# Attention products of batches 2 to 4: one fixed order, raised priority, and projections that start with both of their banks

## The chip, the cores and the metric

One core of one Trainium2 chip runs the kernel. The metric is the device time of one execution in microseconds; lower is better. Three runs of the kernel before gave 902.72, 903.56 and 904.33 us, median 903.56 us.

## The reference

The computation is a linear-attention layer with random features, followed by two dense layers without bias that share one token matrix.

```python
def _attn_ref(q, k, v, omega):            # q, k, v: (4, 8, 576, 64), omega: (128, 64)
    scale = 1.0 / np.sqrt(np.sqrt(D))
    def phi(x):
        proj = np.einsum('bhsd,md->bhsm', x, omega)
        h = proj - np.sum(x * x, axis=-1, keepdims=True) / 2.0
        h = h - np.max(h, axis=-1, keepdims=True)
        return np.exp(h) / np.sqrt(m)
    q_p, k_p = phi(q * scale), phi(k * scale)
    kv = np.einsum('bhsm,bhsd->bhmd', k_p, v)
    z = np.sum(k_p, axis=2)
    num = np.einsum('bhsm,bhmd->bhsd', q_p, kv)
    den = np.einsum('bhsm,bhm->bhs', q_p, z)[..., None] + 1e-06
    return num / den
...
x = attn_out.transpose(0, 2, 1, 3).reshape(2304, 512)
h = x @ w_in;  x = (h * np.clip(h + 3.0, 0.0, 6.0) / 6.0) @ w_out        # first layer, d_ff 2048
h = x @ w2_in; x = (h / (1.0 + np.exp(-1.702 * h))) @ w2_out              # second layer
```

## The kernel before, in words

The four batches are numbered b = 0 to 3 in the code; "batch 2 to 4" in the name of the change are b = 1 to 3. A batch has 576 tokens, handled as 4 blocks of 128 and a rest of 64, the "leftover"; the leftovers of two heads share a tile.

**Attention of one batch** (class `Att`) is a list of steps, and each step is a burst of small products on TensorE. For head h:

- `PJ(h)`, through `project` (L282): the features of k and q. Eight fp32 products with 64 contraction rows each. The two halves of the rows of TensorE work at the same time on two products, one half writing into the first of two PSUM banks and the other into the second; `project` emits second bank, first bank, second bank, and so on, each queued behind the last. VectorE then takes the maxima of each bank (L295), ScalarE the exponentials (L297).
- `QT(h)` (L366): four 128x128 transposes of the q features into one bank, copied out by ScalarE.
- `KV(h)` (L341): ten products of 128 rows by 64 columns that make the 128x65 state into one bank; two products side by side use the two halves of the columns.
- `NU(h)` (L377): eight or ten products of the same 128x64 shape, numerator and denominator into one bank; VectorE divides.
- `XT(i)` (L429): four transposes of a finished pair of heads, whose result is split by ScalarE and VectorE into the operand of the first layer. `PL`, `QTL`, `XTL` do the like for the leftover.

In the trace an fp32 product appears as two records, so a `project` is 16 records, a `KV` 20, a `NU` 16 or 20, a set of transposes 4.

**The first layer** runs in units of one batch n and one 128-wide chunk c of d_ff, 16 units a batch. `emit_h` (L504) makes twelve products of 512 columns at L513 into one bank. ScalarE (L524) and VectorE (L525) form the gate value, ScalarE (L529) and VectorE (L530) split it in two. `emit_o` (L541) comes two units later and makes twelve products at L555 into the four accumulation banks. I call the products of L513 and L555 layer products.

**How the two meet.** Attention of batch n + 1 is interleaved with the layer products of batch n: `side()` (L765) is called four times a unit, and every second call pops attention steps from a list at an even pace. The other call, and the hooks "gate" and "next", place the conversion of the weights and the sums for the second layer on ScalarE, VectorE, GpSimd and the DMA queue. After batch n's units the list is emptied. The attention of batch 0 comes first and has no layer beside it.

**Banks.** Of PSUM's eight banks, four (pool `acc`) belong to the accumulators of `emit_o` and four (pool `psp`, tag "ps") to all else; from b = 1 on, every attention step and every `emit_h` takes its banks from those four.

**What sets the order in the queues.** The program text isn't the order on an engine. The framework's scheduler builds each engine's queue ahead of time over a model of its own: whenever an engine is free in that model it takes the instruction that is ready there and stands first in priority, which is the order of the text. "Ready" includes that a bank is free. `issue_after` (in `behind`, L115) forces an instruction behind a given one of the same engine; `tc.high_priority(offset=n)` ranks an instruction as if it stood n places earlier. On the chip each engine then works through its queue in that order and waits where the data isn't there.

**Order of the steps of one batch** (`att_steps`, L450). With `b >= PAIRED`, the paired order, head h gives `PJ(h)`, for even h from 4 on `XT`, then `QT(h-1)`, then `NU(h-2)` and `KV(h-1)` as one step. Otherwise `PJ(h)`, `NU(h-2)`, `QT(h-1)`, `KV(h-1)` are steps of their own, and `XT` follows for odd h. `PAIRED` is 2, so b = 2 and 3 have the paired order and b = 1 the other.

After the first layer come the two pairs of batches of the second (L856, L873, L1008), which the change doesn't touch.

Of the kernel before, what the change touches and what calls it, by code (L numbers as in the profile page):

```python
# [22 lines left out]
def performer_moe_kernel(  # L23
# [13 lines left out]
    nc = tc.nc  # L37
# [10 lines left out]
    SL = lv.shape[1] // 2  # L48
# [7 lines left out]
    WARM = 8  # L56
    FIRST = 4
    ASIDE = 2
    PAIRED = 2
    HELD = 8  # L60
    AT_X = (0, 0, 0, 0)
    AT_XL = 32
# [23 lines left out]
    ident = const.tile([P, P], F32, name="ident")  # L86
# [28 lines left out]
    def behind(*ins):  # L115
        stack = ExitStack()
        for i in ins:
            if i is not None:
                stack.enter_context(tc.issue_after(i.ins))
        return stack  # L120
# [158 lines left out]
        nc.scalar.copy(hi, ps)  # L279
        nc.vector.tensor_tensor(out=lo, in0=ps, in1=hi.bitcast(F32), op=ALU.subtract)  # L280

    def project(a, ps):  # L282

        last = None
        for n in range(4):
            for half in (1, 0):
                rows = HALVES[half]
                with behind(last):
                    last = nc.tensor.matmul(  # L289
                        out=ps[half][:, n, :], lhsT=a(rows, n), rhs=omt[rows, :], start=True, stop=True  # L290
                    )

# [9 lines left out]
    class Att:  # L302
# [10 lines left out]
        def PL(self):  # L313
            a, self.vl = lqkv.pop(self.b)
            self.el = at.tile([P, 2 * NPAIR, M], F32, tag="el", name="el")
            ps = [bank([P, NPAIR, M], "ps") for _ in HALVES]
            project(lambda rows, i: a[rows, i, :], ps)
            for j, p in enumerate(ps):
                features(p, self.el[:, j * NPAIR:(j + 1) * NPAIR])

        def QTL(self):
            ps = bank([P, NPAIR, P], "ps")
            for i in range(NPAIR):
                nc.tensor.transpose(ps[:, i, :], self.leftover(i, 0), ident)
            self.qtl = at.tile([P, NPAIR, P], F32, tag="qtl", name="qtl")
            nc.scalar.copy(self.qtl, ps)
            shape = [P, NPAIR, D] if self.aside else [SL, NPAIR, 2 * D]
            self.xln = at.tile(shape, F32, tag=f"xln{self.aside}", name="xln")

        def PJ(self, h):  # L330
            a = qkv[self.b, h // 2][0][:, h % 2]
            ps = [bank([P, R, M], "ps") for _ in HALVES]
            project(lambda rows, n: a[rows, n // 2, n % 2, :], ps)
            self.e[h] = at.tile([P, 2, R, M], F32, tag="e", bufs=2, name="e")
            for half, p in enumerate(ps):
                self.feat[h] = features(p, self.e[h][:, half])
# [4 lines left out]
        def KV(self, h):  # L341
            i = h // 2
            vv = qkv[self.b, i][1]
            ps = bank([P, D + 1], "ps")
            for r in range(R):
                for m0 in (0, 64):
                    nc.tensor.matmul(  # L347
                        out=ps[m0:m0 + 64, :],
                        lhsT=self.feature(h, 0, r)[:, m0:m0 + 64],
                        rhs=vv[:, h % 2, r, :],  # L350
                        start=(r == 0),
                        stop=False,
                    )
            for m0 in (0, 64):
                nc.tensor.matmul(
                    out=ps[m0:m0 + 64, :],
                    lhsT=self.leftover(i, 1)[:, m0:m0 + 64],
                    rhs=self.vl[:, h % 2, i, :],
                    start=False,
                    stop=True,  # L360
                )
            kv = at.tile([P, D + 1], F32, tag="kv", bufs=4, name="kv")
            nc.scalar.copy(kv, ps)
            self.kv[h] = kv

        def QT(self, h):  # L366
            ps = bank([P, R, P], "ps")
            for r in range(R):
                nc.tensor.transpose(ps[:, r, :], self.feature(h, 1, r), ident)  # L369
            t = at.tile([P, R, P], F32, tag="qpt", bufs=2, name="qpt")  # L370
            if self.b == 0:
                nc.vector.tensor_copy(t, ps)
            else:
                nc.scalar.copy(t, ps)
            self.qt[h] = t

        def NU(self, h):  # L377
            i = h // 2
            t = self.qt.pop(h)
            kv = self.kv[h]  # L380
            if h % 2 == 0:
                self.xt[i] = at.tile([P, R, 2, D], F32, tag="xt", bufs=1, name="xt")
            ps = bank([P, 6, D + 1], "ps")
            for r in range(R):
                for s0 in (0, 64):
                    nc.tensor.matmul(  # L386
                        out=ps[s0:s0 + 64, r, :],
                        lhsT=t[:, r, s0:s0 + 64],
                        rhs=kv,
                        start=True,  # L390
                        stop=True,
                    )
            if h % 2:
                for e in range(2):
                    nc.tensor.matmul(
                        out=ps[HALVES[e], R, :] if self.aside else ps[0:SL, R + e, :],
                        lhsT=self.qtl[:, i, HALVES[e]],
                        rhs=self.kv.pop(2 * i + e),
                        start=True,
                        stop=True,  # L400
                    )
            dst = self.xt[i][:, :, h % 2, :]
            if h % 2 and self.aside:
                self.norm(ps[:, 0:R + 1, :], (dst, self.xln[:, i:i + 1, :]), P)
                return
            self.norm(ps[:, 0:R, :], (dst,), P)
            if h % 2:
                self.norm(ps[0:SL, R:R + 2, :], (self.xln[:, i].rearrange("p (h d) -> p h d", h=2),), SL)
# [20 lines left out]
        def XT(self, i):  # L429
            t = self.xt.pop(i)  # L430
            ps = bank([P, R, P], "ps")
            for r in range(R):
                nc.tensor.transpose(ps[:, r, :], t[:, r].rearrange("p h d -> p (h d)"), ident)
            o = ps.rearrange("p r s -> p (r s)")
            split(self.x[:, 0, i, :], self.x[:, 1, i, :], o)

        def XTL(self):
            ps = bank([P, NPAIR, SL], "ps")
            for i in range(NPAIR):
                if self.aside:  # L440
                    for e in HALVES:
                        nc.tensor.matmul(
                            out=ps[e, i, :], lhsT=self.xln[e, i, :], rhs=ident[e, e], start=True, stop=True
                        )
                else:
                    nc.tensor.transpose(ps[:, i, :], self.xln[:, i], ident[0:SL, 0:SL])
            c0 = self.b * SL
            nc.scalar.copy(self.xl[:, :, c0:c0 + SL], ps)

# [300 lines left out]
                prefetch_w()  # L750
    banks[0] = "ps"

    units = [(n, c) for n in range(B) for c in range(NC)]
    fetches = [
        (n * NC + u, k_, c)
# [489 lines left out]
```

## Time and profile before

| what | value |
|---|---|
| median of 3 runs | 903.56 us (902.72 to 904.33) |
| the profiled execution | 906.58 us |
| its span, first to last instruction | 904.8 us |
| PE busy | 886.0 us (98%) |
| VectorE, ScalarE, GpSimd busy | 554.3, 478.0, 322.6 us |
| mean granted TensorE clock | 0.998 of full |

The rows come from the profiled execution. PE is TensorE's products, PEld its weight loads, DVE VectorE, ACT ScalarE, POOL GpSimd, SP the engine that issues DMAs. An instruction's line number is that of the kernel before. The ends of products are modelled, so how long a burst holds TensorE is best read from its start to the start of what comes next.

### The profile page before, as it was taken

The page shows a single profiled execution, that of the slowest core. Times are in us where ns is not written, and L with a number is a line of the kernel's source. Part 1 is how long each engine was busy: PE and PEld are TensorE (multiplying, and loading weights), DVE is VectorE, ACT ScalarE, POOL GpSimd, SP SyncE. Part 2 cuts the span into 40 slices and gives each one's busy share as a digit, 9 for nine tenths or more (in the row PEclk, how much of TensorE's full clock was granted, in tenths as well). Part 3 has the DMA queues.
Part 4 walks back from the last instruction along what each step waited for, and adds up shares of the span by engine and source line. Part 5 has one row for each costly group of instructions (what it writes and reads, how often), then busy time and mean ns, then how long its engine had stood idle before and what let it go on. Part 6 is the DMA issues. An engine that isn't in the chain of part 4 may idle for free.

```text
span 904.8 us, 16525 instructions
## 1 busy us (share of the span) xinstructions
PE 886.0 (98%) x6344; PEld 757.1 (84%) x6344; DVE 554.3 (61%) x952; ACT 478.0 (53%) x973; POOL 322.6 (36%) x257
## 2 busy tenths in 40 slices
PE   8899999999999999999999999999999999999998
PEld 6667777788788778878888888878999888899998
DVE  5887688473754736475573343666887343368785
ACT  5887677376664666656553343444545232245452
POOL 0122222044636565475673121877000243440000
PEclk9999999999999999999999999999999999999999
DMA  6677669698888987778857325999889644565562
GB/s 209 226 248 270 234 239 316 245 329 282 286 275 288 342 304 290 233 276 288 314 204 256 128 98 206 349 400 356 277 288 354 233 170 162 180 174 153 158 204 82
DMA packets 74416, 224.57 MB, mean 248 GB/s; under 512 B 7521, under 2 KB 13793, under 8 KB 74337
## 3 DMA queue, kind: packets, MB, share of 16 engines
q1 hardware_dynamic: 73872, 223.12, 71.1%
q8 instruction: 50, 0.82, 0.4%
q10 hardware_dynamic: 464, 0.39, 0.2%
q14 instruction: 30, 0.24, 0.1%
HBM read 160.57 MB, written 62.91 MB: 247 GB/s over the span
## 4 chain that ended last, share of the span: by engine, by line
PE 82%; DVE 8%; ACT 6%; issue 1%; POOL 1%; DMA 1%; DVEq 0%; SPq 0%; ACTq 0%; POOLq 0%
PE o L1008 19%; PE o L555 18%; PE ps L513 18%; PE h L856 16%; PE hl L873 3%; PE ps L289 2%; ACT e L297 2%; DVE w L236 2%; PE ps L386 1%; PE ps L347 1%; ACT wtop L213 1%; DVE mx L295 1%; DVE wtop L221 1%; PE ps L369 1%; DVE gs L530 1%
## 5 line engine op out<-in xcount | busy, mean ns | idle before, releaser
L513 PE MATMUL ps<-x,wss 128*128 128x512 f32 x768 | 195.5, 399 | 2.5 <-ACT el L297 1.1
L1008 PE MATMUL o<-wss,gs 128*128 128x256 f32 x1512 | 173.9, 277 | 0.2 <-DVE gs L977 0.2
L1008 PEld LDWEIGHTS o<-wss,gs 128*128 128x128 f32 x1512 | 173.4, 188 | 0.9 <-DVE gs L977 0.6
L513 PEld LDWEIGHTS ps<-x,wss 128*128 128x128 f32 x768 | 140.9, 189 | 35.0 <-ACT wss L239 3.1
L856 PE MATMUL h<-xo,wss 128*128 128x512 f32 x672 | 158.5, 391 | 0.9 <-DVE t L889 0.9
L856 PEld LDWEIGHTS h<-xo,wss 128*128 128x128 f32 x672 | 123.9, 188 | 27.5 <-DVE t L889 1.8
L228 POOL TENSOR_TENSOR w<-w,wpow 128x1024 f32<-128x1024 f32 x32 | 69.2, 2162 | 204.6 <-DVE wpow L225 166.7
L525 DVE SCALAR_TENSOR_TENSOR ga<-ga,ps 128x512 f32<-128x512 f32 x80 | 50.1, 632 | 121.1 <-ACT ga L524 121.1
L899 POOL TENSOR_TENSOR g<-g,c 128x512 f32<-128x512 f32 x48 | 64.7, 1349 | 164.0 <-ACT g L898 163.8
L976 ACT CAST gs<-g 128x512 fp32r<-128x512 f32 x112 | 69.6, 622 | 80.3 <-PE o L1008 49.3
L555 PE MATMUL o<-gs,wsh 128*128 128x512 f32 (+1 forms) x480 | 110.4, 374 | 1.2 <-ACT gs L529 1.0
L555 PE MATMUL o<-gs,wss 128*128 128x512 f32 (+1 forms) x480 | 109.5, 374 | 0.2 <-ACT gs L529 0.2
L253 POOL TENSOR_TENSOR wsn<-w,wsn 128x512 fp32r<-128x512 f32 x64 | 86.6, 1367 | 63.5 <-ACT wsn L252 63.5
L977 DVE TENSOR_TENSOR gs<-g,gs 128x512 fp32r<-128x512 f32 x112 | 79.9, 716 | 33.6 <-ACT gs L976 32.3
L524 ACT ACTIVATE ga<-ps,three 128x512 f32<-128x512 f32 x80 | 51.4, 650 | 86.5 <-PE ps L513 86.0
L555 PEld LDWEIGHTS o<-gs,wsh 128*128 128x128 f32 x480 | 82.2, 188 | 17.6 <-ACT gs L529 1.4
L555 PEld LDWEIGHTS o<-gs,wss 128*128 128x128 f32 x480 | 82.4, 188 | 15.8 <-ACT gs L529 0.4
L297 ACT ACTIVATE e<-ps,mx 128x128 f32<-128x128 f32 x220 | 61.1, 396 | 23.5 <-DVE mx L295 23.3
L530 DVE TENSOR_TENSOR gs<-ga,gs 128x512 fp32r<-128x512 f32 x80 | 62.5, 791 | 16.5 <-ACT gs L529 14.7
L898 ACT ACTIVATE g<-c 128x512 f32<-128x512 f32 x48 | 30.3, 632 | 60.2 <-DVE c L889 60.2
L529 ACT CAST gs<-ga 128x512 fp32r<-128x512 f32 x80 | 46.0, 580 | 27.8 <-DVE ga L525 27.4
L252 ACT CAST wsn<-w 128x512 fp32r<-128x512 f32 x64 | 38.3, 620 | 39.5 <-DVE w L236 13.2
(132 smaller groups left out, 1102.7 us busy)
## 6 DMA issues: line engine op xcount, KB each, us to landing
wss<-left SPq DMA_DIRECT2D x56, 512.0 KB, 3.9
wss<-ws0i SPq DMA_DIRECT2D x48, 512.0 KB, 4.9
wraw<-in_w_in_dram SPq DMA_DIRECT2D x32, 512.0 KB, 5.4
wraw<-in_w_out_dram SPq DMA_DIRECT2D x32, 512.0 KB, 6.3
left<-wsn SPq DMA_DIRECT2D x32, 512.0 KB, 3.7
wss<-ws0o SPq DMA_DIRECT2D x24, 512.0 KB, 4.6
ws0i<-wss SPq DMA_DIRECT2D x16, 512.0 KB, 3.3
wss<-sumsa SPq DMA_DIRECT2D x16, 512.0 KB, 3.5
```

What stands on the lines that cost most here:

```text
L228: nc.gpsimd.tensor_tensor(out=w, in0=w, in1=q, op=ALU.mult)
L253: nc.gpsimd.tensor_tensor(out=s[:, :, 1], in0=t, in1=s[:, :, 0].bitcast(F32), op=ALU.subtract)
L297: act = nc.scalar.activation(out=e[:, r, :], in_=ps[:, r, :], func=AF.Exp, bias=mx[:, r:r + 1])
L513: nc.tensor.matmul(out=ps, lhsT=w[:, wi, kk, :], rhs=x[:, xi, kk, :], start=(m == 0), stop=(m == 3 * NK - 1),)
L524: nc.scalar.activation(out=g, in_=ps, func=AF.Relu, bias=three)
L530: gate[1] = nc.vector.tensor_tensor(out=s[:, 1, :], in0=g, in1=s[:, 0, :].bitcast(F32), op=ALU.subtract)
L555: nc.tensor.matmul(out=ps[:, e, :], lhsT=w[:, wi, cols], rhs=s[:, gi, :], start=(c == 0 and m == 0 and e == 0), stop=(c == NC - 1 and m == ...
L856: nc.tensor.matmul(out=ps, lhsT=s[:, wi, q, :], rhs=xop[q, op][:, xi], start=(first and m == 0), stop=(m == 5), skip_group_check=not first,)
L899: mul = eng.tensor_tensor(out=g, in0=g, in1=src, op=ALU.mult)
L976: split_ins[0] = nc.scalar.copy(hi, g)
L977: split_ins[1] = nc.vector.tensor_tensor(out=lo, in0=g, in1=hi.bitcast(F32), op=ALU.subtract)
L1008: last_row[0] = nc.tensor.matmul(out=out, lhsT=s[:, gi, d * P:(d + 1) * P], rhs=w[:, wi, :], start=(start and m == 0), stop=(stop and m == 2),
```

## The change

Three things, all in the attention of b = 1 to 3; the switch `queued[0]` is None while batch 0's attention is emitted.

- Every TensorE instruction of the attention goes through a new helper `mm`. It queues the instruction behind the attention instruction before it, so that they stand on TensorE in the order of the program among themselves (layer products may still stand between them), and ranks it 40 places earlier.
- In `project`, for b > 0, ScalarE first copies one column of a constant into the first bank and then, queued behind that, one into the second. The products overwrite both, so each waits for the copies, and the first product starts only when both banks are to be had. The copies have no raised rank.
- `PAIRED` goes from 2 to 1: b = 1 takes the paired order too.

```diff
-    PAIRED = 2
+    PAIRED = 1
+    RAISE = 40
...
-    def project(a, ps):
+    queued = [None]
+
+    def mm(f, *a, **args):
+        if queued[0] is None:
+            return f(*a, **args)
+        with behind(*queued[0]), tc.high_priority(offset=RAISE):
+            queued[0] = [f(*a, **args)]
+        return queued[0][0]
+
+    def project(a, ps, both=False):

         last = None
+        if both:
+            with behind(nc.scalar.copy(ps[0][:, 0, 0:1], three)):
+                nc.scalar.copy(ps[1][:, 0, 0:1], three)
         for n in range(4):
             for half in (1, 0):
                 rows = HALVES[half]
                 with behind(last):
-                    last = nc.tensor.matmul(
+                    last = mm(
+                        nc.tensor.matmul,
                         out=ps[half][:, n, :], lhsT=a(rows, n), rhs=omt[rows, :], start=True, stop=True
                     )
...
-            project(lambda rows, i: a[rows, i, :], ps)
+            project(lambda rows, i: a[rows, i, :], ps, self.b > 0)
...
-                nc.tensor.transpose(ps[:, i, :], self.leftover(i, 0), ident)
+                mm(nc.tensor.transpose, ps[:, i, :], self.leftover(i, 0), ident)
...
-                    nc.tensor.matmul(
+                    mm(
+                        nc.tensor.matmul,
                         out=ps[m0:m0 + 64, :],
...
+    queued[0] = []
     units = [(n, c) for n in range(B) for c in range(NC)]
```

The cut parts wrap the remaining products of `PJ`, `KV`, `QT`, `NU`, `XT` and `XTL` in `mm` in the same way.

## Rows read from the trace of the kernel before

**Rows 1.** The page's first part: engine, busy us (share of span), instructions.
```profile
PE 886.0 (98%) x6344; PEld 757.1 (84%) x6344; DVE 554.3 (61%) x952; ACT 478.0 (53%) x973; POOL 322.6 (36%) x257
```

**Rows 2.** Windows: stretch, length, busy us by engine, PEclk granted clock, DMA share, GB/s.
```profile
53.90:175.00 121.10, 119.24 (x856) 92.36 (x856) 89.09 (x181) 86.02 (x169) 27.90 (x13) 1.00 0.74 261
175.00:293.00 118.00, 117.85 (x895) 95.09 (x895) 67.38 (x114) 72.92 (x162) 60.16 (x51) 1.00 0.81 284
293.00:411.00 118.00, 115.91 (x877) 92.55 (x876) 66.98 (x112) 72.38 (x162) 65.58 (x56) 0.99 0.81 289
318.00:320.00 2.00, 2.00 (x6) 1.51 (x7) 0.58 (x1) 2.00 (x9) 1.92 (x3) 0.51 0.85 288
```

**Rows 3.** Timeline of PE, projections: start, us, engine, line, out<-in, shapes, records.
```profile
53.94 0.48 PE L289 MATMUL ps<-omt,lqk 64*128 64x128 f32 x2
...
226.24 1.16 PE L289 MATMUL ps<-omt,qk 64*128 64x128 f32 x16
227.33 0.73 PE L555 MATMUL o<-gs,wsh 128*128 128x512 f32 x2
...
338.16 0.48 PE L289 MATMUL ps<-omt,qk 64*128 64x128 f32 x2
338.58 3.06 PE L555 MATMUL o<-gs,wss 128*128 128x512 f32 x12
341.56 1.16 PE L289 MATMUL ps<-omt,qk 64*128 64x128 f32 x14
342.65 0.66 PE L369 MATMUL ps<-ident,e 128*128 128x128 f32 x4
...
387.58 0.48 PE L289 MATMUL ps<-omt,qk 64*128 64x128 f32 x2
```

**Rows 4.** Timeline of PE: one head of b = 1, then one of b = 2.
```profile
78.24 0.69 PE L386 MATMUL ps<-kv,qpt 128*64 128x65 f32 x16
78.86 0.66 PE L369 MATMUL ps<-ident,e 128*128 128x128 f32 x4
...
80.37 0.69 PE L347 MATMUL ps<-v,e 128*64 128x65 f32 x16
...
81.11 2.57 PE L513 MATMUL ps<-x,wss 128*128 128x512 f32 x10
...
213.62 0.69 PE L386 MATMUL ps<-kv,qpt 128*64 128x65 f32 x16
...
214.82 0.48 PE L289 MATMUL ps<-omt,qk 64*128 64x128 f32 x2
```

**Rows 5.** Timeline of PE, b = 1: a numerator cut by layer products.
```profile
156.35 0.57 PE L386 MATMUL ps<-kv,qpt 128*64 128x65 f32 x12
156.85 2.60 PE L513 MATMUL ps<-x,wss 128*128 128x512 f32 x10
159.38 0.34 PE L386 MATMUL ps<-kv,qpt 128*64 128x65 f32 x4
159.65 1.20 PE L555 MATMUL o<-gs,wss 128*128 128x512 f32 x4
```

**Rows 6.** Timeline of PE: twelve layer products after transposes, before other layer products.
```profile
376.67 2.99 PE L513 MATMUL ps<-x,wss 128*128 128x512 f32 x12
379.50 1.30 PE L555 MATMUL o<-gs,wsh 128*128 128x512 f32 x5
```

**Rows 7.** Timeline of PE and DVE, start of b = 3; in brackets idle before, and releaser.
```profile
311.59 0.48 PE L289 MATMUL ps<-omt,qk 64*128 64x128 f32 x2
...
314.82 0.67 DVE L525 SCALAR_TENSOR_TENSOR ga<-ga,ps 128x512 f32<-128x512 f32 x1
...
315.55 1.16 PE L289 MATMUL ps<-omt,qk 64*128 64x128 f32 x14 [0.74 <-DVE ga L525]
...
317.82 4.61 PE L513 MATMUL ps<-x,wss 128*128 128x512 f32 x12 [1.11 <-ACT el L297]
```

**Rows 8.** Groups by line and shape, ACT, 53.9 to 411 us: busy us, mean ns.
```profile
L363 ACT COPY kv<-ps 128x65 f32<-128x65 f32 x24 | 5.4, 225 | 3.7 <-PE ps L355 3.5
```

More of the change, by code (lines that the diff above doesn't have):

```diff
@@ L332, in PJ @@
             ps = [bank([P, R, M], "ps") for _ in HALVES]
-            project(lambda rows, n: a[rows, n // 2, n % 2, :], ps)
+            project(lambda rows, n: a[rows, n // 2, n % 2, :], ps, self.b > 0)
             self.e[h] = at.tile([P, 2, R, M], F32, tag="e", bufs=2, name="e")
@@ L354, in KV @@
             for m0 in (0, 64):
-                nc.tensor.matmul(
+                mm(
+                        nc.tensor.matmul,
                     out=ps[m0:m0 + 64, :],
@@ L368, in QT @@
             for r in range(R):
-                nc.tensor.transpose(ps[:, r, :], self.feature(h, 1, r), ident)
+                mm(nc.tensor.transpose, ps[:, r, :], self.feature(h, 1, r), ident)
             t = at.tile([P, R, P], F32, tag="qpt", bufs=2, name="qpt")
@@ L385, in NU @@
                 for s0 in (0, 64):
-                    nc.tensor.matmul(
+                    mm(
+                        nc.tensor.matmul,
                         out=ps[s0:s0 + 64, r, :],
@@ L394, in NU @@
                 for e in range(2):
-                    nc.tensor.matmul(
+                    mm(
+                        nc.tensor.matmul,
                         out=ps[HALVES[e], R, :] if self.aside else ps[0:SL, R + e, :],
@@ L432, in XT @@
             for r in range(R):
-                nc.tensor.transpose(ps[:, r, :], t[:, r].rearrange("p h d -> p (h d)"), ident)
+                mm(nc.tensor.transpose, ps[:, r, :], t[:, r].rearrange("p h d -> p (h d)"), ident)
             o = ps.rearrange("p r s -> p (r s)")
@@ L441, in XTL @@
                     for e in HALVES:
-                        nc.tensor.matmul(
+                        mm(
+                        nc.tensor.matmul,
                             out=ps[e, i, :], lhsT=self.xln[e, i, :], rhs=ident[e, e], start=True, stop=True
@@ L445, in XTL @@
                 else:
-                    nc.tensor.transpose(ps[:, i, :], self.xln[:, i], ident[0:SL, 0:SL])
+                    mm(nc.tensor.transpose, ps[:, i, :], self.xln[:, i], ident[0:SL, 0:SL])
             c0 = self.b * SL
```

## The prediction

> **What bounds the kernel now.** I read the page's busy shares first: PE is busy for 886.0 of 904.8 us and no other engine for more than 61% [rows 1]. So a microsecond of PE time saved is a microsecond of the end, as long as PE finds work at once. Next the windows of the three stages in which attention of b = 1, 2, 3 lies beside the first layer: 53.9 to 175, 175 to 293 and 293 to 411 us. PE is idle there for 1.9, 0.15 and 2.1 us (length less busy), while ScalarE has 35 to 46 us free in each and VectorE 32 to 51 [rows 2]. All of the change lies in these 357 us. Busy isn't well used, though, so I went through PE's timeline for what each burst holds.
>
> A whole projection lasts from 226.24 to 227.33, 1.09 us for 16 records [rows 3]. But at 338.16 only 2 records go out, the first product, whose partner had no bank yet; then come twelve layer products, and the other 14 records take 341.56 to 342.65, 1.09 us again [rows 3]. The lone product costs 0.42 us and shortens the rest by nothing, since the seven left still need four slots in time. The timeline between 53.9 and 411 us has nine such cuts, from 53.94 to 387.58 [rows 3].
>
> **The change part by part.** (A) Both banks first. Nine cuts go, at 338.58 - 338.16 = 0.42 us each [rows 3]: 3.8 us less.
>
> (B) The paired order for b = 1. In a head of b = 1 the numerator holds PE for 0.62 us (78.24 to 78.86), transposes follow, and the state holds it for 0.74 (80.37 to 81.11), 1.36 together; in b = 2 the same two bursts stand side by side and take 213.62 to 214.82, 1.20 us [rows 4]. Eight heads at 0.16: 1.3 us less. The list of b = 1 falls from 41 steps to 35; its four loads keep their places behind the same `KV` within a few us, nothing is added to SP's queue, and the `XT` that comes a head later still has the rest of the batch ahead of it. I cost these moves at nothing.
>
> (C) The chain with raised rank. In b = 1 five bursts are cut in two by layer products. The numerator at 156.35 takes 0.50 us, then, after ten layer products, 0.27 more (159.38 to 159.65), 0.77 against 0.62 for a whole one [rows 4, 5]. Five cuts at 0.15: 0.75 us less. The later batches have no such cuts and already stand in the order that the chain prescribes, so there it forbids nothing that happens now.
>
> (D) Fewer visits to the layer products. Twelve of them between two bursts of split shapes take 338.58 to 341.56, 2.98 us [rows 3]; behind transposes, which use the whole array as they do, 376.67 to 379.50, 2.83 us [rows 6]. A visit thus costs 0.15 us. In the timeline b = 1 has 32 visits, b = 2 and 3 have 24 and 23. With (B) and (C) I give b = 1 eight fewer: 1.2 us. What the raised rank merges in all three stages lies between nothing and 7 us (rival three); I take four visits, 0.6 us, because each burst after a projection is ready early, but the projection itself waits for copies that aren't raised.
>
> (E) What the copies cost. Three batches with nine projections and two copies each are 54 instructions on ScalarE. No row shows a copy of one column; the nearest is 128x65, 225 ns [rows 8], so 0 to 12 us of ScalarE, which has 126 us free in the three stages [rows 2]. On PE the two in line cost 0.45 us where the second bank is free late and no layer product is ready. The ends are 0 and 27 x 0.45 = 12.2 us. In the trace, late banks come nine times, and PE ran out of layer products in front of one of them [rows 7]; I take three exposed cases, 1.35 us. The wait itself is now on ScalarE: behind a copy that waits for a bank stand the exponentials, the gate casts of L529 and the weight casts of L239, and behind those the layer products. Under their cover nothing is lost; without it rival one begins.
>
> The Trainium skill (ScalarE: Activation LUTs, section "What ACT_TABLE_LOAD costs") gives an ACTIVATE with immediate scale and bias 186 ns plus 0.833 ns an element, from which I estimate 187 ns for one column; the exposed term would then be 1.1 us. No row of this case shows it.
>
> Sum: 3.8 + 1.3 + 0.75 + 1.2 + 0.6 - 1.35 = 6.3 us less. The profiled execution took 906.58 us (span 904.8 and 1.8 around it), so it would take 900.3. It ran 3.0 us above the median; carried to the median of 903.56 that is **897.3 us**.
>
> **Rivals.** One, slower: bank starvation at the starts of the batches. `PL` and the second projection follow each other there and want all four banks. At the start of b = 3 this already happens: the second projection has one bank from 311.59 on, the last bank is released by VectorE's step that ends at 315.49, PE idles 0.74 us before 315.55 and 1.11 us before 317.82 [rows 7]. Behind it the granted clock is 0.51 in 318 to 320, about the lower level of 1.2 GHz, after PE had been idle in two short pieces [rows 2, 7], and twelve layer products take 4.61 us in place of 3.06 [rows 3, 7], so one such place costs 0.74 + 1.11 + 1.55 = 3.4 us. After the change the first bank stays empty while ScalarE waits for the second, and the raised products take the next free one ahead of `emit_h`. Three new places like this would cost 10.2 us: 897.3 + 10.2 = 907.5. It decides from 8.1 us, between two and three places. Against it: the starts of b = 1 and 2 have the same need and show no such wait, and the whole stage of b = 2 idles 0.15 us. Chance 0.17.
>
> The skill speaks for this rival twice. TensorEngine Tiling (Array Packing), section "Gotcha 1: PSUM Pressure", says that row tiling raises the need for banks since different row tiles write to different ones; the wait at 315.55 agrees. Perfetto Trace Analysis, section "Tensor Engine Instruction (MATMUL, LD_WEIGHTS)", calls ScalarE's queue strictly first in, first out; no row here shows what a blocked copy holds up.
>
> Two, the change doesn't do what it says: layer products still stand between the chained bursts of b = 1, because the numerator, the state and the transposes wait for banks one by one, and only (A) is had. The copies then show in each of the nine late places, 9 x 0.45 = 4.05 against 3.8 us. Time 903.8. For it: all the bursts of a head share four banks with `emit_h`. Against it: b = 2 and 3 pair these bursts today with the same banks. Chance 0.18.
>
> Three, the raised rank works fully: projection, transposes, numerator and state of a head run without layer products between them. Of 79 visits some 27 are left, and 52 at 0.15 us are 7.8 us in place of the 1.8 in (D): 897.3 - 6.0 = 891.3. Against it: such a run wants five banks of four. Chance 0.12.
>
> **How the numbers follow.** The forecast has 0.53. Its own range is 893.5 to 900.5: up by the copies' exposure going to nine places (4.05 - 1.35 = 2.7) and a little more, down by the 1.35 going to nothing and half of rival three's merging. Over all cases I give 890 to 906: rival three and two lie inside, rival one's two-stall form (904.1) too; outside are its heavier half and a tenth of rival three's side. What this kernel's measurement can tell from no change is 0.2%, 1.8 us. Faster by more than that: 0.53 and 0.12, 0.65. Within it: rival two, 0.18. Slower: rival one, 0.17.
>
> **What the profile after should show.** (A) no projection with a first stretch of 2 records; the projections' stretches all of 16. (B) in b = 1 a numerator of 16 or 20 records with a state of 20 right behind it, 1.20 us for the two. (C) no bursts of 2, 4, 6, 12 or 14 records of the 128x64 shape. (D) about 24 visits in b = 1 where there are 32, and the stage of b = 1 shorter by about 4 us, those of b = 2 and 3 by about 1 us each. (E) 54 new ScalarE copies at or below 225 ns, and PE idle for no more than 1.5 us beyond now in the 357 us. Wrong would be the forecast if PE's waits name ScalarE's new copies or `el` of L297 at several batch starts, with a granted clock near half behind them; if b = 1 still shows its transposes between numerator and state; or if stages after 411 us, which the change leaves alone, move by more than 1 us.

## The result, and the profile after

The changed kernel takes 914.35 us (median of 4 runs, 912.53 to 915.82); the kernel before, beside it, 903.34 us (902.72 to 904.33). The ratio is 1.0123, 95% interval 1.0102 to 1.0144: 11 us slower, where 6.3 us faster was forecast.

The page of the profile after, first part, as in [rows 1]. PE is busy 3.3 us less, in a span 8.7 us longer (the gap is smaller than that of the medians, since the profiled execution of before ran 3 us above its median):

```profile
PE 882.7 (97%) x6344; PEld 756.6 (83%) x6344; DVE 562.8 (62%) x952; ACT 482.2 (53%) x1027; POOL 320.6 (35%) x257
```

Windows of after: the three of [rows 2], then the handover from batch 0 to the first layer, and two places with a low granted clock (columns as in [rows 2]):

```profile
53.90:175.00 121.10, 114.82 (x839) 91.19 (x839) 96.16 (x188) 87.12 (x187) 27.83 (x13) 0.96 0.75 257
175.00:293.00 118.00, 117.44 (x885) 93.92 (x884) 66.22 (x113) 73.15 (x177) 53.78 (x44) 1.00 0.79 275
293.00:411.00 118.00, 113.34 (x854) 90.64 (x853) 68.00 (x108) 73.40 (x180) 63.52 (x56) 0.99 0.80 285
30.00:80.00 50.00, 38.53 (x306) 29.17 (x305) 35.99 (x76) 34.23 (x82) 11.83 (x6) 0.90 0.71 236
64.00:72.00 8.00, 7.05 (x41) 5.70 (x42) 4.79 (x10) 3.76 (x10) 2.12 (x1) 0.57 0.80 254
323.00:327.00 4.00, 3.85 (x21) 3.24 (x22) 2.74 (x5) 3.22 (x14) 3.65 (x5) 0.57 1.02 384
```

The handover window in the kernel before:

```profile
30.00:80.00 50.00, 46.34 (x407) 35.38 (x404) 41.02 (x84) 40.01 (x91) 12.39 (x6) 1.00 0.71 240
```

PE's idle time in the three stages is 6.3, 0.6 and 4.7 us where it was 1.9, 0.15 and 2.1 [rows 2]. Most of the loss begins earlier than the stages that I had looked at: from 30 to 80 us PE idles 11.5 us in place of 3.7, and does 306 records in place of 407.

The change does most of what it says. PE's timeline of after: a projection in one piece, and a numerator with its state right behind it in b = 1 (in two other heads there, at 104.06 and 166.33, layer products still stand between the two).

```profile
87.01 1.16 PE L289 MATMUL ps<-omt,qk 64*128 64x128 f32 x16
...
95.29 0.69 PE L289 MATMUL ps<-kv,qpt 128*64 128x65 f32 x16
95.80 0.64 PE L289 MATMUL ps<-v,e 128*64 128x65 f32 x16
96.27 0.29 PE L289 MATMUL ps<-lv,el 128*64 128x65 f32 x4
96.48 2.79 PE L532 MATMUL ps<-x,wss 128*128 128x512 f32 x11
```

The two take 95.29 to 96.48, 1.19 us (1.20 in b = 2 before [rows 4]). No projection in the three stages begins with two records, and layer products are visited 68 times up to the end of b = 3's attention, at 419 us, not 79 (66 up to 411). The copies, by line and shape on ScalarE:

```profile
L296 ACT COPY ps<-three 128x1 f32<-128x1 f32 x27 | 4.9, 181 | 0.7 <-DVE x L281 0.5
L297 ACT COPY ps<-three 128x1 f32<-128x1 f32 x27 | 4.5, 167 | 0.2
```

I split the time from the first instruction to the first product of the second layer, 549.4 us before and 557.5 after, in three: PE's idle time (the sum of the gaps in its timeline), what a low clock costs (the sum of length times one less the granted clock), and the rest, which I call work. (Idle time inside a stretch of low clock is counted in both, so work comes out 0.5 us too low in after.) Idle goes from 13.8 to 25.1 us, the low clock's cost from 1.7 to 6.8, work from 533.9 to 525.6. So a saving of about 8 us is there, and about 16 are given back. Behind that point the two kernels differ by 0.6 us.

**Where it is lost.** By the start of chunk 4 of the first layer, after is 8.4 us behind (81.1 against 72.7 us). PE's timeline there:

```profile
54.05 3.84 PE L532 MATMUL ps<-x,wss 128*128 128x512 f32 x9 [2.95 <-ACT wss L240]
57.73 0.60 PE L287 MATMUL acc<-ident,xt 128*128 128x128 f32 x4
...
59.00 2.37 PE L532 MATMUL ps<-x,wss 128*128 128x512 f32 x9 [0.29 <-ACT x L280]
64.95 3.78 PE L574 MATMUL o<-gs,wsh 128*128 128x512 f32 x8 [3.59 <-ACT ps L297]
```

Two waits of 2.95 and 3.59 us, and behind both the products run slower: nine take 3.84 us from 54.05 and 2.37 from 59.00, eight take 3.78 us from 64.95, and the clock in 64 to 72 is 0.57. The name L297 at the second wait is that of the copy that ended last; these products read `gs`, whose cast ends at 64.90. VectorE's timeline of after, then of before (L237, L309, L431 and L544 of after are L236, L295, L413 and L525 of before):

```profile
43.97 1.29 DVE L237 TENSOR_TENSOR w<-w,wtop 128x512 f32<-128x512 f32 x2 [2.31 <-POOL w L229]
...
45.78 1.28 DVE L309 TENSOR_REDUCE mx<-ps 128x4 f32<-128x512 f32 x2
...
52.65 1.29 DVE L237 TENSOR_TENSOR w<-w,wtop 128x512 f32<-128x512 f32 x2 [1.99 <-POOL w L229]
53.86 0.15 DVE L431 TENSOR_SCALAR den<-acc 128x4 f32<-128x4 f32 x1
...
61.22 1.89 DVE L544 SCALAR_TENSOR_TENSOR ga<-ga,ps 128x512 f32<-128x512 f32 x3 [0.22 <-ACT ga L543]
```

```profile
42.11 1.28 DVE L295 TENSOR_REDUCE mx<-ps 128x4 f32<-128x512 f32 x2
...
44.50 1.29 DVE L236 TENSOR_TENSOR w<-w,wtop 128x512 f32<-128x512 f32 x2 [0.45 <-POOL w L228]
...
48.24 0.16 DVE L413 TENSOR_SCALAR den<-acc 128x4 f32<-128x4 f32 x1
...
53.87 1.28 DVE L525 SCALAR_TENSOR_TENSOR ga<-ga,ps 128x512 f32<-128x512 f32 x2
```

The additions that finish a chunk's weights wait for GpSimd. In after they stand ahead of the maxima of b = 1's first projection and of batch 0's last denominators, so these come late (45.78 for 42.11, 53.86 for 48.24), and with them ScalarE's exponentials, the last state, the last transposes, and the operand of the first layer. Then the gates of three chunks fall due together, on ScalarE behind weight work:

```profile
60.49 1.85 ACT L543 ACTIVATE ga<-ps,three 128x512 f32<-128x512 f32 x3 [1.27 <-PE ps L532]
62.22 1.15 ACT L240 CAST wss<-w 128x512 fp32r<-128x512 f32 x2
63.25 1.15 ACT L214 ACTIVATE wtop<-wraw 128x1024 bf16<-128x1024 bf16 x1
64.28 0.62 ACT L548 CAST gs<-ga 128x512 fp32r<-128x512 f32 x1
64.78 0.18 ACT L297 COPY ps<-three 128x1 f32<-128x1 f32 x1
```

The second place is the start of b = 3, where [rows 7] has two short waits. Timeline of after, three engines:

```profile
321.14 0.67 DVE L544 SCALAR_TENSOR_TENSOR ga<-ga,ps 128x512 f32<-128x512 f32 x1
321.18 0.16 ACT L296 COPY ps<-three 128x1 f32<-128x1 f32 x1
321.90 0.62 ACT L548 CAST gs<-ga 128x512 fp32r<-128x512 f32 x1 [0.57 <-DVE ga L544]
322.43 0.61 ACT L253 CAST wsn<-w 128x512 fp32r<-128x512 f32 x1
...
322.95 0.15 ACT L297 COPY ps<-three 128x1 f32<-128x1 f32 x1
323.15 1.75 PE L289 MATMUL ps<-omt,qk 64*128 64x128 f32 x16 [2.49 <-ACT ps L297]
```

VectorE frees the bank at 321.81, but the copy that the projection waits for stands behind two casts on ScalarE and runs at 322.95. PE idles 2.49 us, and the clock in 323 to 327 is 0.57.

### The profile page after: what moved, and what is told of

It is laid out like the page before. It is cut to its first block, busy times and chain, and to the rows that moved or that the text cites. A ratio compares the mean times of both kernels' runs of the same rounds, so it can differ in the third digit from the quotient of the medians.

```text
span 913.5 us, 16614 instructions
## 1 busy us (share of the span) xinstructions
PE 882.7 (97%) x6344; PEld 756.6 (83%) x6344; DVE 562.8 (62%) x952; ACT 482.2 (53%) x1027; POOL 320.6 (35%) x257
## 4 chain that ended last, share of the span: by engine, by line
PE 68%; DVE 14%; ACT 8%; POOL 4%; issue 3%; DMA 3%; SPq 0%; DVEq 0%; POOLq 0%; ACTq 0%
PE o L1028 19%; PE ps L532 14%; PE o L574 13%; PE h L876 13%; PE ps L289 4%; DVE w L237 3%; PE hl L893 2%; POOL w L229 2%; ACT e L311 2%; DVE gs L549 2%; DVE mx L309 2%; DVE wtop L222 2%; ACT wtop L214 1%; DVE ga L544 1%; DVE wmag L218 1%
## 5 line engine op out<-in xcount | busy, mean ns | idle before, releaser
L544 DVE SCALAR_TENSOR_TENSOR ga<-ga,ps 128x512 f32<-128x512 f32 x80 | 50.1, 632 | 113.4 <-ACT ga L543 113.3
L574 PE MATMUL o<-gs,wss 128*128 128x512 f32 (+1 forms) x480 | 107.1, 372 | 0.0
L549 DVE TENSOR_TENSOR gs<-ga,gs 128x512 fp32r<-128x512 f32 x80 | 66.8, 844 | 23.0 <-ACT gs L548 21.4
```

The lines of the kernel that those rows point to most:

```text
L544: nc.vector.scalar_tensor_tensor(out=g, in0=g, scalar=6.0, in1=ps, op0=ALU.min, op1=ALU.mult)
L549: gate[1] = nc.vector.tensor_tensor(out=s[:, 1, :], in0=g, in1=s[:, 0, :].bitcast(F32), op=ALU.subtract)
L574: nc.tensor.matmul(out=ps[:, e, :], lhsT=w[:, wi, cols], rhs=s[:, gi, :], start=(c == 0 and m == 0 and e == 0), stop=(c == NC - 1 and m == ...
```

## The experiments

Five theories. One: the order in VectorE's queue, weight additions ahead of attention or gates, costs the time. Two: the copies themselves do. Three: the raised rank takes banks from the layer products. Four: none has a price; any edit makes the scheduler draw the queues anew over its model, and the queues of before are a good draw. Five: the single buffer `wtop` of the conversion sets the pace.

The table gives medians and ratios, and from one profile of each kernel how far it is behind the first profile of before: gained or lost up to chunk 4, in the rest of b = 1's stage, in b = 2's, in b = 3's (a stage ends with the first layer product of the next batch, b = 3's with that of its own batch); and the split in idle, low clock and work. Line e9 shows how much one profile can be trusted: before against itself, -3.3 us, of it -2.5 in b = 3, where the wait of 0.74 us in [rows 7] and the low clock behind the two waits were missing.

| kernel | median us | ratio, 95% interval | to chunk 4 | rest of b = 1 | b = 2 | b = 3 | idle | clock | work |
|---|---|---|---|---|---|---|---|---|---|
| after | 914.35 | 1.0123, 1.0102 to 1.0144 | +8.4 | -1.4 | -0.6 | +1.7 | +11.3 | +5.1 | -8.3 |
| e1 copies only | 913.55 | 1.0104, 1.0086 to 1.0121 | +2.9 | +2.7 | -0.6 | +1.8 | +9.3 | +1.7 | -4.2 |
| e2 chain only | 916.48 | 1.0138, 1.0123 to 1.0153 | +4.2 | +3.9 | +2.0 | +0.6 | +5.8 | +3.4 | +1.6 |
| e3 rank not raised | 908.92 | 1.0051, 1.0031 to 1.0072 | +0.7 | -0.8 | +1.0 | +1.9 | +9.0 | +1.7 | -7.9 |
| e4 b = 2, 3 only | 906.61 | 1.0025, 1.0005 to 1.0044 | +0.4 | 0.0 | -0.6 | -0.5 | +3.2 | -1.7 | -2.1 |
| e5 handover mended | 912.75 | 1.0102, 1.0075 to 1.0129 | +1.1 | +1.1 | +1.8 | +1.6 | +10.2 | 0.0 | -4.6 |
| e6 paired only | 905.88 | 1.0031, 1.0015 to 1.0047 | +0.5 | -1.3 | +2.1 | -2.5 | +0.6 | 0.0 | -1.7 |
| e7 control, pace | 910.38 | 1.0078, 1.0056 to 1.0100 | +2.6 | +6.3 | -1.0 | -2.9 | +4.3 | +1.7 | -1.1 |
| e8 from head 2 on | 910.89 | 1.0077, 1.0052 to 1.0102 | +0.5 | +2.9 | -0.5 | +0.7 | +5.9 | +5.1 | -7.3 |
| e9 before again | 903.41 | one run | -1.0 | +0.1 | 0.0 | -2.5 | -1.9 | 0.0 | -1.4 |
| e10 control, buffer | 917.46 | 1.0138, 1.0111 to 1.0164 | +8.8 | +4.6 | -0.9 | -2.7 | +7.7 | +3.4 | -1.2 |
| e11 e5 and buffer | 924.81 | 1.0211, 1.0176 to 1.0247 | +10.0 | +8.8 | -0.5 | +1.4 | +18.3 | +8.5 | -6.9 |
| e12 e3 and buffer | 923.83 | 1.0209, 1.0170 to 1.0248 | +6.0 | +12.6 | -0.6 | +1.1 | +16.9 | +11.9 | -9.7 |
| e13 control, gate | 911.44 | 1.0082, 1.0067 to 1.0097 | -0.1 | +8.1 | -0.9 | -2.9 | +5.6 | -1.7 | +0.3 |
| e14 e5 and gate | 916.63 | 1.0140, 1.0119 to 1.0161 | +3.9 | +1.4 | +2.8 | -0.8 | +12.3 | 0.0 | -4.8 |
| e15 e8 and gate | 911.90 | 1.0088, 1.0068 to 1.0107 | +0.1 | +1.5 | +2.7 | +1.8 | +9.7 | +1.7 | -5.3 |
| e16 e3 and gate | 914.48 | 1.0121, 1.0104 to 1.0138 | +2.8 | -0.4 | +2.4 | +0.2 | +12.8 | -1.7 | -6.1 |
| e17 after and pace | 916.28 | 1.0137, 1.0113 to 1.0162 | +1.3 | +6.7 | -0.3 | +1.0 | +11.4 | +3.4 | -6.1 |
| e18 e3 and pace | 916.70 | 1.0146, 1.0129 to 1.0163 | +1.2 | +8.4 | -0.6 | +1.5 | +13.7 | +5.1 | -8.4 |

**Parts alone: e1 (copies), e2 (chain and rank), e3 (the change without the rank), e6 (paired order).**

```diff
 e1:  -    PAIRED = 1        +    PAIRED = 2      -    queued[0] = []
 e2:  -    PAIRED = 1        +    PAIRED = 2      -    project(..., self.b > 0)   +    project(..., False)
 e3:  -    RAISE = 40        +    RAISE = 0
 e6 (of before):  -    PAIRED = 2        +    PAIRED = 1
```

> Only the one-column copies, for b = 1 to 3; no chain, no raised rank, old order of steps for b = 1. Theory one, the queues at the handover: the changed kernel loses 8 us where batch 0's attention ends and the first layer begins, since in its VectorE queue the weight adds (which wait for GpSimd) stand ahead of the maxima of b = 1's first projection, and behind those wait the exponentials, the state copy of batch 0's last head and its last transposes. In this kernel's queue the maxima stand ahead of the adds, so the handover is within 2 us of before and ten cut projections at 0.42 us are gone: 898 to 903 us. Theory two, the copies themselves: ScalarE's waits for banks hold up what stands behind them, whatever else is changed: 909 us or more. Theory three, the raised rank takes banks from the layer products: not in here, 899 us.

> Only the chain with raised rank; no copies, old order of steps for b = 1. Theory one (order at the handover): the maxima stand ahead of the first adds here, but the second pair of adds stands ahead of the last step of batch 0's division, so a part of the loss may show, 0 to 4 us, and the cut projections stay: 903 to 908 us. Theory two (copies): 901 to 903 us, no loss without copies. Theory three (raised rank): 909 us or more.

> The changed kernel with a raise of 0 in place of 40: chain, copies and the paired order of b = 1 stay. Theory one (order at the handover): the maxima stand ahead of the adds in this queue, so the 8 us at the handover go: 898 to 904 us. Theory two (copies): 910 us or more. Theory three (raised rank): the loss goes, 897 to 902 us; it parts from theory one by the place: with three the gain is spread over the stages, with one it is at the handover before 75 us.

> Only the paired order for b = 1. Theories one and two: no loss at the handover, whose VectorE order is that of the kernel before, and numerator and state side by side in b = 1: 900 to 903 us. Theory four: 905 us or more, with new waits in the stage of b = 1.

Every part alone is slower than before, and the prices don't make a sum: 9 us for the copies, 12 for chain and rank, 3 for the paired order, 11 for all (each is the ratio less one, times 904 us). The work of e1 falls by 4.2 us, which is about term (A), 3.8, by itself. Chain and rank alone (e2) save no work: it rises by 1.6 us. Without the rank the handover is whole, and the change costs 4.6 us in place of 11.

**The change from b = 2 on, or from head 2 of b = 1 on: e4, e8.**

```diff
 e4:  -    PAIRED = 1        +    PAIRED = 2
      -    project(..., self.b > 0)   +    project(..., self.b > 1)      # chain likewise from b = 2
 e8:  +            if (self.b, h) == (1, 2):
      +                queued[0] = []                                    # chain and copies from here
      -    project(..., self.b > 0)   +    project(..., queued[0] is not None)     -    queued[0] = []   # before the units
```

> The whole change for b = 2 and 3 alone, b = 1 as before. All three theories put most of the loss into different places. Theory one: all but 1 to 2 us of it is at the handover to b = 1, which is untouched here: b = 2 gives 0.6 us, the start of b = 3 costs 1.6, so 903 to 906 us. Theories two and three hold in b = 2 and 3 as well, with two thirds of the loss: 908 us or more.

> The whole change, but chain, raise and copies begin with head 2 of b = 1, so that the handover (the projections of heads 0 and 1 and of the leftover) is queued as before. Theory one: all of the handover's 8 us go, the interior of b = 1 gains 1 to 3, b = 3 loses 1 to 2: 901 to 906 us. Theory two: most of the copies are still there, 910 us or more. Theory four: 906 to 912 us, with the handover as before and waits later in b = 1.

With b = 1 left alone the change is within 0.5% of before, but not faster. With the handover left alone the time is lost later in b = 1, in one wait of 3.3 us near 156 us, again behind additions that wait for GpSimd.

None of the first three theories has the first four runs in its ranges. Theory one missed all four (e4 by 0.6 us), theory two e2, e3 and e4, theory three e1, e3 and e4. Theory one then missed e5 to e8 and e13 as well.

**The handover mended: e5.**

```diff
-            with behind(dve if l == 1 else None):
+            with behind(dve if l == 1 else hold.get((l, c))):
...
+            if (self.b, h) == (1, 0):
+                hold[0, 1] = self.feat[h][1]      # additions of chunk 1: behind the first maxima of b = 1
...
+            if (self.b, i) == (0, NPAIR - 1):
+                hold[0, 2] = lo                   # of chunk 2: behind batch 0's last split
```

> The changed kernel with two edges more on VectorE: the weight adds of chunk 1 stand behind the maxima of b = 1's first projection, those of chunk 2 behind the split of batch 0's last transposes. Nothing else differs. Theory one (order at the handover): the handover falls from 8.4 to 2 us behind the kernel before, and as the later stages are what they are in the changed kernel the time is 906 to 909 us. Theory two (copies on ScalarE hold up what stands behind them): 912 to 916 us. Theory four (the kernel before has a lucky order, and any other one that the scheduler draws over its model loses some us, each at other places): the handover is mended, but the losses come up elsewhere, 908 to 914 us.

VectorE's timeline of e5 has the order that the edges ask for, maxima and last denominators ahead of the additions (L238, L310 and L434 are L237, L309 and L431 of after):

```profile
42.63 1.28 DVE L310 TENSOR_REDUCE mx<-ps 128x4 f32<-128x512 f32 x2
43.83 1.28 DVE L238 TENSOR_TENSOR w<-w,wtop 128x512 f32<-128x512 f32 x2
...
49.86 0.16 DVE L434 TENSOR_SCALAR den<-acc 128x4 f32<-128x4 f32 x1 [0.63 <-PE acc L288]
...
52.73 1.28 DVE L238 TENSOR_TENSOR w<-w,wtop 128x512 f32<-128x512 f32 x2
```

PE's timeline of e5: no wait of 2.95 or 3.59 us, but new ones, one a chunk, later in the stage (the last of five).

```profile
52.15 5.25 PE L537 MATMUL ps<-x,wss 128*128 128x512 f32 x18 [0.28 <-ACT x L281]
57.44 2.14 PE L579 MATMUL o<-gs,wsh 128*128 128x512 f32 x8
...
157.44 2.11 PE L579 MATMUL o<-gs,wss 128*128 128x512 f32 x8 [1.19 <-ACT gs L553]
```

The handover's loss falls from 8.4 to 1.1 us. An edge also makes the scheduler draw the queues anew, so e5 alone doesn't part the order from a redraw; the other traces do. In no kernel but after do the additions of chunk 2 stand ahead of batch 0's last denominators, and where a quite different edit takes that order away (e17 below) the handover's loss is 1.3 us. So the order in VectorE's queue is the cause of after's loss at the handover. It isn't the only way to lose time there: e2, e10 and e12 lose 4.2 to 8.8 us without it, and e11, which has both edges of e5, loses 10.0. And e5's median falls by 1.6 us only: by the profiles 2.5 us are lost again in the rest of b = 1's stage and 2.4 in that of b = 2.

**Controls, no part of the change in them: e7, e9, e10, e13.**

```diff
 e7:   -    pace[:] = len(todo), 0, 8 * (n > 0)       +    pace[:] = len(todo), 0, 2 if n == 0 else 8
 e9:   none
 e10:  -    tag=f"wtop{l and c % 2}"                  +    tag=f"wtop{c % 2}"
 e13:  +    if n == 0 and c > 1:
       +        hold[0, c + 1] = formed               # additions of chunk c + 1: behind the gate product of chunk c
      # and the additions read hold, as in e5
```

> The kernel before with its attention steps of b = 1 asked for two calls of side later (late_by 2 in place of 0 for n = 0); no part of the change is in it and no work is added. Theories one to three say nothing against it: 902 to 905 us. Theory four: a control that draws another order, so 906 to 914 us, with waits of PE in the stage of b = 1 at new places.

> The kernel before, profiled once more, since its first profiled execution is 3 us above its median. If the wait at the start of b = 3 (1.85 us idle and a low clock behind it) belongs to the kernel, it is there again; if it is chance of that one execution, the span is about 901 to 902 us and b = 3 starts without it.

> The kernel before with two buffers in place of one for the upper half of the weights while they are converted (tile wtop, first layer), so that ScalarE can read chunk c + 1 before VectorE has added chunk c. Theory five (in the stage of b = 1 the conversion of the weights, one chunk after the other through one buffer, sets the pace as soon as PE gets ahead): little here, PE idles 1.9 us in 80 to 180: 901 to 904 us. Theory four (any other order costs): 905 us or more.

> The kernel before with one thing forced: in the first layer's units of batch 0, the additions on VectorE that form the weights of chunk c + 1 (c from 2 on) are queued behind the gate product of chunk c, where the scheduler is free to put them ahead of it. Theory one (the additions wait for GpSimd and hold up the gate behind them in VectorE's queue): the kernel before has few such places, about 4.7 us of PE idle between 30 and 180 us, so it gains at most 2 us: 901 to 904. Theory four (any other queue than that of before loses, since the scheduler's order is drawn over a model): 907 to 911, as with the other small disturbance that left the change out (910.4).

The three edits cost 7 to 13 us. e10 speaks against theory five, and so do e11 and e12 below: with the second buffer all three are slower than before, by 12 us or more. e13 removes just the order that I held to be the cause, at each chunk from the third on, and loses 8 us; one of its places, three engines (lines one higher than in before):

```profile
103.35 0.69 ACT L525 ACTIVATE ga<-ps,three 128x512 f32<-128x512 f32 x1 [2.43 <-PE ps L514]
...
103.78 1.29 DVE L296 TENSOR_REDUCE mx<-ps 128x4 f32<-128x512 f32 x2 [2.13 <-PE ps L290]
104.51 2.18 ACT L298 ACTIVATE e<-ps,mx 128x128 f32<-128x128 f32 x8 [0.47 <-DVE mx L296]
104.99 0.68 DVE L526 SCALAR_TENSOR_TENSOR ga<-ga,ps 128x512 f32<-128x512 f32 x1
...
106.53 0.67 ACT L532 CAST gs<-ga 128x512 fp32r<-128x512 f32 x1
...
107.25 2.11 PE L558 MATMUL o<-gs,wss 128*128 128x512 f32 x8 [2.39 <-ACT gs L532]
```

The gate of a chunk goes from ScalarE to VectorE to ScalarE to PE. Here maxima stand ahead of its second step (104.99 where the first ends at 104.04) and eight exponentials ahead of its third (106.53 where the second ends at 105.67). No weight addition is in the way. The waits only moved: theory one is right for the handover, and too narrow for the stage.

**Both together: e11, e12 (second `wtop` buffer), e14, e15, e16 (gate order), e17, e18 (pace).** Each is one form of the change with the edit of a control.

> The changed kernel with the two edges on VectorE (as in the run with those alone) and two buffers for wtop. Theory five: PE's waits for gate casts and weights in 80 to 180 us, 5.1 us with one buffer, fall under 2: 906 to 909 us. Theory four: they move, 909 to 914 us.

> The changed kernel with a raise of 0 and two buffers for wtop. Theory five: the 3.9 us of PE idle in 80 to 180 us fall by half or more, 903 to 906 us. Theory four: 906 to 912 us, with other waits.

> The whole change, with the two VectorE edges at the handover from batch 0 (912.75 without more), and now also the additions of chunk c + 1 behind the gate product of chunk c in batch 0's units. Theory one: PE's waits on the gate casts between 120 and 160 us (five of 0.3 to 1.2 us, 3 us in all) and the idle time of 5.1 us in 80 to 180 go to about 2 us, and the work saved (4.6 to 8 us) shows: 904 to 909. Theory four: the waits move elsewhere in the stage, its idle stays at 4 to 7 us, and the time stays at 910 to 915.

> The change from head 2 of b = 1 on, the handover left as before (910.89 without more), with the additions of chunk c + 1 behind the gate product of chunk c in batch 0's units. Theory one: the 3.3 us wait near 156 us on a gate cast behind such additions goes, idle in 80 to 180 us falls from 6.3 to about 3, and the time to 904 to 908. Theory four: it stays at 908 to 913 with the idle time in other places.

> The whole change without the raised rank (908.92 without more), with the additions of chunk c + 1 behind the gate product of chunk c in batch 0's units. It had 3.9 us idle in 80 to 180 us and 6.7 in 180 to 420. Theory one: the first falls by 1.5 to 2.5 us, the second, where nothing is edited, stays within 1 us: 906 to 908. Theory four: the first doesn't fall, or the second changes by more than 1 us although nothing is edited there: 907 to 914.

> The whole change, and the same small shift of pace in b = 1 that cost the kernel before 7 us by itself (its attention steps are dealt out a little faster). If the change and the shift each have a price of their own, they add: 914 + 7 = 921. Theory four, that every edit only makes the scheduler draw other queues, among which the queue of before is a good one: they don't add; the handover from batch 0, which the shift also redraws, loses something else than 8.4 us, and the time lies anywhere between 906 and 918.

> The whole change without the raised rank (908.92 without more), and the same shift of pace. With prices of their own: 909 + 7 = 916. Theory four: no sum; between 904 and 915, with PE's work some 6 to 8 us below that of before as in every form that keeps the both-banks copies and the chain, and idle time that varies by several us.

Theory one missed e14, e15 and e16: none got faster, e14 and e16 got slower by 4 and 6 us. The pace runs say most. e17 should be 921 by prices that add and is 916.3: the handover's loss is 1.3 us although nothing was done for it, and b = 1's whole stage loses 8.0 us, where after alone loses 7.0 and the control alone 8.9. So b = 1's losses don't add there. e18 is 916.7, the 916 of the sum and above the range of theory four; but e3, to which the control was added there, had no loss in b = 1, so no second one was there to be added. The raised rank, worth 5.4 us between after and e3, is worth nothing between e17 and e18.

Over all seven pairs, prices that add are right for some: by the ratios e12, e16 and e18 lie within 2 us of the sum of their two edits, e11 2.6 us below it, but e14, e15 and e17 4.0 to 6.4 us below. Theory four's ranges held for e5 to e8, e10, e15 and e17; e13, e14, e16 and e18 lie 0.4 to 1.7 us above them, e11 and e12 some 11 and 12.

One loss does repeat. PE's timeline at the start of b = 3, in e3, then in e18:

```profile
317.87 1.37 PE L289 MATMUL ps<-omt,qk 64*128 64x128 f32 x16 [2.49 <-ACT ps L297]
```

```profile
325.69 2.08 PE L289 MATMUL ps<-omt,qk 64*128 64x128 f32 x16 [2.49 <-ACT ps L297]
```

All thirteen kernels with the copies in b = 3 have this wait, of 2.14 us (e8) to 2.50; in the seven traces without them PE waits 1.11 us at a time at most at the start of b = 3. In the controls and e6, which have no copies, the stage of b = 3 takes 2.5 to 2.9 us less than in the first profile of before; in after, e1, e3, e17 and e18 it takes 1.0 to 1.9 more; e4, e14 and e16 lie between. (e2 has no copies either, but shows the double wait of [rows 7] again, 0.86 and 1.11 us.) The copies cost about 4 us there, idle and low clock together, where a low clock follows. In e4, e14 and e16 none does, and the price is the wait alone. PE's timeline of e16 (lines one higher than in after), and its window:

```profile
321.59 1.16 PE L290 MATMUL ps<-omt,qk 64*128 64x128 f32 x16 [2.50 <-ACT ps L298]
```

```profile
318.00:328.00 10.00, 7.50 (x55) 6.26 (x56) 5.35 (x8) 7.64 (x27) 7.90 (x9) 1.00 1.00 379
```

A second, smaller loss goes with the chain: near the end of b = 3's stage a layer product waits for the exponentials, 1.24 us before 402.88 in after and 0.82 to 1.66 us in every other kernel with the chain in b = 3. In e1, which has the copies alone, it is 0.48 us, and in before, e6 and the controls no such wait reaches 0.3.

No kernel was faster than before; the nearest are e4 and e6.

## Why the prediction was wrong

**(A) to (D), the work.** The sum was right: 3.8 + 1.3 + 0.75 + 1.8 = 7.65 us were foretold, about 8 measured (8.3, or 6.9 against the second profile of before). Its terms are only in part shown one by one: (A) was 3.8 and is 4.2 in e1, (B) was 1.3 and is 1.7 in e6, eleven visits fewer where twelve were counted on; but (C) and the rank's part of (D) save nothing in e2, where they stand alone. Two profiles of one kernel differ by 1.4 us in work, so that the sum came so near is in part luck.

**The step that failed** is the condition under the sum: a microsecond of PE time saved is one of the end "as long as PE finds work at once". (A) to (D) have no term for what the new order does to the queues of VectorE and ScalarE. (B) says "I cost these moves at nothing", (C) that in the later batches the chain "forbids nothing that happens now". The runs showed 11.3 us more of idle time and 5.1 us more of low clock; the sum had 1.35 us for the two together. The list of steps, the chain and the rank decide what the scheduler finds ready at each moment, and so the order in the in-order queues of the other engines; I followed PE's queue and SP's alone. I had read that the program text isn't the order on an engine, and took that for a remark on PE. The condition holds only while each gate passes ScalarE and VectorE in time, and in the stage of b = 1 the weights of the next chunk are made on the same engines meanwhile. That VectorE has 32 us free and ScalarE 35 there [rows 2] says nothing on it: a free share doesn't help what stands behind a waiting instruction.

The loss can't be laid on one part. (B)'s moves alone (e6) lose 0.5 us up to chunk 4 and gain 1.3 in the rest of b = 1. The 8.4 us at the handover go when the rank goes (e3, 0.7), but also when the rank stays and the pace is shifted (e17, 1.3).

**(E), "Under their cover nothing is lost".** The size of a copy was right: 181 and 167 ns, below the 225 of [rows 8]. The Trainium skill (ScalarE: Activation LUTs, section "What ACT_TABLE_LOAD costs") led to 187 ns as an estimate; the trace is a little below. The exposure of 1.35 us was too low: about 4 us at one place. (E) asked what stands behind a copy that waits for its bank; here the copy itself stood in ScalarE's queue behind other work while its bank was already free, for 1.14 us of the 2.49. The Trainium skill (Perfetto Trace Analysis, section "Tensor Engine Instruction (MATMUL, LD_WEIGHTS)") has ScalarE's queue strictly in order, and the trace agrees: the bank is free at 321.81, the copy runs at 322.95, behind two casts.

**Rival one** had the right side, 907.5, and at the start of b = 3 the right place, near its price of 3.4 us. It was priced for three such places and got one; the larger part of the loss, 7 us by the end of b = 1, came at the handover through VectorE, of which no rival spoke. **Rival two** (the change doesn't do what it says) and **three** (full merging) fell by the counts above.

**The signs.** A low clock behind waits of PE was named as a sign against the forecast, and is there; so is L297, but at one start of a batch, and at the handover as a releaser in name only. Stages after 411 us were to stand within 1 us, and do (0.6).

**What is settled, and what isn't.** Shown: the saving in work; the order in VectorE's queue as the cause at the handover (e5, e17, and the queues of the others); the copies' price at the start of b = 3 (thirteen kernels with them, seven traces without); that edits with no part of the change lose as much in b = 1 (e7, e10, e13), and that the losses there need not add (e17). Theory four fits most of this, though not all of its ranges held, and it is what is left rather than what was isolated: of seventeen edited kernels none was faster than before, and why just the queues of before lose so little was not found. Theory two holds for one place, theory three for none that stays when something else is moved.

## What to carry to other kernels

Where a scheduler builds the queues over a model, an edit on one engine reorders the others too; run a control edit of the same size that should change nothing, before a gain of 1% is believed, and put its loss into the sum as a term. Follow the shortest chain that passes several in-order engines (here the gate: ScalarE, VectorE, ScalarE, PE) and name what may come to stand ahead of each step; free shares of the engines don't bound that. A write that only reserves a buffer makes its user wait for what stands ahead of it on the engine that writes it (here two casts, 1.14 us).

## What the runs showed of the hardware

Waits of PE of nearly the same length were followed by different clocks. Behind 2.49 us in after, the granted clock in 323 to 327 is 0.57, near the lower level of 1.2 GHz, and the sixteen records of the projection take 1.75 us; behind 2.50 us at the same place in e16 the clock in 318 to 328 is 1.00 and they take 1.16. And e13 waits 2.39 us before 107.25, its eight products then take 2.11 us, and its window is at the full 2.4 GHz:

```profile
80.00:180.00 100.00, 91.39 (x669) 69.18 (x668) 69.66 (x146) 64.67 (x122) 21.45 (x10) 1.00 0.74 255
```

A low clock thus can't be foretold here from the length of one wait, and its cost (1.7 to 3.4 us a time in after, over half of the wait ahead of it) makes single profiles scatter.
